# Steps from the 189th on in another order, with three masks more on VectorE and three fewer on GpSimd

## The chip, the cores and the metric

The kernel runs on one core of one Trainium2 chip. The metric is the device time of one execution in microseconds. The core has five engines with a queue of instructions each, in the order in which the program recorded them: TensorE (PE; its weight loads, PEld, are shown apart), VectorE (DVE), ScalarE (ACT), GpSimd (POOL) and SyncE (SP, which issues DMAs). An instruction waits at the head of its queue until what it depends on is done, and everything behind it in that queue waits too.

## The reference

Sliding-window attention with four sink tokens, then a perceptron with a squared relu over the 4 x 768 tokens:

```python
# q, k, v: 4 batches x 8 heads x 768 x 64, n_sink 4, window 128
keep = (pos[None, :] < n_sink) | ((rel >= 0) & (rel < window))   # rel = pos[:, None] - pos[None, :]
scores = np.where(keep, np.matmul(q, k.transpose(0, 1, 3, 2)) / np.sqrt(64), -1000000000.0)
a = np.exp(scores - np.max(scores, axis=-1, keepdims=True))
a = a / (np.sum(a, axis=-1, keepdims=True) + 1e-09)
x = np.matmul(a, v).transpose(0, 2, 1, 3).reshape(3072, 512)
h = np.maximum(x @ w_in, 0.0)          # w_in: 512 x 2048
out = (h * h) @ w_out                  # w_out: 2048 x 512
```

## The kernel before

The program is a table of 992 steps (`P.ops`): each is a small function that issues a few instructions on one engine. A string, `ORDER`, lists the numbers of the steps in the order in which `Plan.run` records them; a letter behind a number names the engine (p, d, a, g for PE, DVE, ACT, POOL; without a letter it is the first that the step allows), and `+0` or `+1` chooses between two pools of PSUM banks (`den` and `att`, two slots each). Slots of SBUF pools are given out in the order of the string too: eight `expm` slots (exponentials and the copies `t`), three `r`, four `sg`, two `osb`. So the string fixes each engine's queue and which slot a step takes; waits follow from the data and from the slots.

Attention of a batch b goes in three blocks s of 256 queries, and a block in two halves of two head pairs. For each half there are four kinds of step. *Scores* (L592 to L613) multiply k by q into `ps` in PSUM. *Expo* (L630, ScalarE) writes exp to `expm` as bf16. *Domask* (L635) zeroes what lies outside the window: in block 0 a product with `mask0` on VectorE (L639); in the others either a product with `tri` on VectorE (L642, one instruction of 1024 columns) or two selects on GpSimd (L218, 512 columns each). *Values* (L678) multiply by v and the sinks into `po`; *norm* (L694, L695, VectorE) divides into `xn_sb`. The choice of L635 to L643 is

```python
elif e == "dve":
    y = x.rearrange("p h (i c) -> p (h i) c", i=2)
    nc.vector.tensor_mul(y, y, tri.rearrange("p (o a) c -> p o (a c)", o=1).to_broadcast(
        [128, 4, 256]))
else:
    y = x.rearrange("p h (i g c) -> p g (h i) c", i=2, g=2)
    for i in range(2):
        triangles(y[:, i], i, 4)
```

The result is transposed to `xT` by TensorE and copies (b = 0, part of 1) or by DMA (`turn_x`); *spread* (L833) copies it into `xd`.

The first layer is done plainly for batch 0 (`layer1`, products L762, squares L785 and L787). From batch 1 on it is done with seven products in place of eight (Strassen's scheme in Winograd's form): sums `xs` of the input (L854) and `wi` of the weights, then `quad` (L867), seven products L892 into two PSUM banks `pm` (each four or eight loads of weights). Out of a quad come copies `t` of a product (*kept*, L192 on ScalarE or L194 on VectorE), *bounded* forms `r` = max(pm + t, 0) (L942, always VectorE), one relu (L967 ScalarE or L969 VectorE), and two *squares* into `gT_sb` (L915 ScalarE or L917 VectorE). A product that overwrites a bank waits for the copy or bounded form that reads it.

The second layer is plain for one block of batch 0 and otherwise again seven products: `layer2_chain` (L1194), products L1239 into `py`; ahead of them four sums of blocks of `gT_sb` on VectorE (L1213: s1 to `sg`, s3 in place in `gT_sb`, s2 and s4 to `sg`), behind them the quarters of the result to `osb`, as copies (L192 or L194) or additions (L1253), and one store. The third quarter's copy frees the region of `py` that the next product writes. The last block of batch 3 runs `layer2_fast` (L1035: sums L1058, products L1100 and others), interleaved with the chain of the block before.

Of the kernel before, what the change touches and what calls it, by code (L numbers as in the profile page):

```python
# [18 lines left out]


ORDER = """
990 1 0 2 7 8 9 10 11 12 13 14 15 16 17 18 56d 60a 55d 991+0 3 19 57+0 61d 20 5 6 4 62+1 65 59a 67+0 58a 21 64d 89d
63a 68+0 75+1 88d 69 70 76+1 22 71+0 77 23 72 73 78 24 94a 79+1 90+0 93d 92a 95+1 80 91d 81 96a 74 100+0 82 101+0 25
26 102 83+1 97d 66 84d 27 104 85 110+1 111+0 103g 86d 152+1 112 28 113d 105d 98+0 99 153 106+0 108 114 115d 154a 116+1
118 29 160+1 109 161 162a 107 30 119 117 120+0 31 155d 163a 122 121d 123d 32 168+0 156+1 331 33 172+0 157 169 164+1
170a 165 34 35 158d 173 166a 124+1 125a 127+0 36 159d 176+1 129a 177 126d 174a 140+1 133+1 37 128d 171d 142 136 180+1
181 282+0 38 178d 167d 137d 132+0 141+1 182a 130+0 39 283 40 144 143d 41 134 42 43 332 284 285 131 145d 146+0 175a 147
135g 278 179a 286 138+1 139 287 288 148+0 150 334 151d 44 149a 279 183d 289 184+1 290 185 193+0 280 281 200+0 201 291
194 45 204+1 196+0 202 46 203 205 198a 186 197 207a 293 206 187+0 199a 216+0+0 47 48 195a 217 49 188d 234+1+0 50 235
190+0 219 208+0 87 292 237 209 295 191 218 297+0 189 220 51 336 52 212 53 210a 294 211 255+0 252+1 254 299 298 256 54  # L30
253a 257 444 223+0+1 333 238d 445 192a 226 304 213 224 221+0 312 222 300 241+1+0 301 214+0 296 244 215 302 225 446
303d 242 306 260+0+0 236 462 263 307 314 337 316+0 245d 243d 315 227 308 313 447 318 319 464 246+0 261 247 239+0 448
240 320 321 228+0 475 322d 317 229 258+0 335 259 325 449 450 310 326 230+0 451 231 452 232 248+0 233 249a 327 250 251a
323 309 305 343+1 359+1 339 338 344 467 340 345 341 360 463 329 311 453 324 328 346 465 347 361 362 363 267+1+1 348
349 350 364 268 342 365d 270 351d 366 367 375+0 352 376 377 354 368 454 355 468 356d 370 369a 357 455 391+0 456 379
264 457 262 466 458 265+0 271 393 353 459 378 269 371 392 395 358a 266 372 272+0 373 381 380 382 474 374a 397 394 273
274+0 383d 276 277 396 275a 384 469 407 386 485+0+0 388d 718 472 387 470 460 486 398 410 461 408 389 412+1 488 471
478+1+0 409 399 473 385 479 400 487 330 413 688 402 414 428+0 404 401 403 405 430 416 429 418 432 406a 489 530+0 481
415 390 417 431 419 532 689 526 411 490+0 434 420 433 435 528 421 423 491 436 437 707 482 527 422a 533 424 480 534 690
708 476+0 477 425 439 440 441 691 535 442 531 483+1 426 529 484 443a 536 494+0+0 537 438a 497 692 427 495 568+0 545  # L40
539 540 570 564 566 492 693 694 695 542 498d 501+0+0 502 565 696 541 493 571 504 697 706 538 572 698 543 569 709
517+0+1 518 546 699 573 544 547 520 700 575 503d 510+0+0 701 574 549+0 496d 583 711 576 567 577 584 578 521d 513 505
579 585 551 581 506+0 552 580 507 514 511 586 512d 553 519 713 588+0 499+0 710 500 554 702 703 555d 515+0 516 522+0
589 719 550 590 712 523 591 745+0+0 748 592 558 556 548 560 746 738+0+0 741 594d 557 593 587 595 559 562 739 561
722+0+0 747 596d 714 604+0 749d 725 597 606 599 605 600 726 601 608 607 715 508 509 723 602 524 716 525 717 656+1 657
598 720+0 658 609 620 721 659 610 622 640+0 750+0 724 611 642 612 621 641 751 613 742 603a 660 662 740 615 644 623 646
614 727+0 616 704 661 617 663 563 643 645 618 647 619 672+0 664 667 665 648 651 649 728 582 674 668 673 669 650 676
670 743+0 652 666a 675 744 653 624+1 678 671a 677 654 626 679 625 729+1+0 680 730 628 770 681 655 630 683 774+0 771
732 684 627 775 685 686 629 772 776 754+0+1 682a 755 731 631 777 687 733 773 632 734+0 735 778 635 779 757 705 761+1+0
633 637 636 781 752 758 780d 634 762 638 756 639a 736 793+0 783 789 764 790 784 759+0 737 791 785 795 760 763 782 765  # L50
794 827 828 800 832+1 766+0 786 787 767 848+0 788 850d 829 833 808 796 834 835 830 849 797 768 836 838d 810 851 753
798 837 852 812+1 792 839 853 799 854 855 856 769 801 802 804 840d 859 803 841 857 831 814 843 815 858 842a 866 844
861 805d 816 845 811 809 806 860 817 868+0 813 862 864 846 819 865 818 863 869 870 884+1 867 871 821 872 885 874 823
886d 873 875 822 847 876 916+0 824 887 888 917 889 932 825 877 878 879 890 934 820 918 880 919 920 900+1 807 902 881d
882 933 891 921 883a 901 892 904 936+0 922d 938 906 903 923 905 893 924d 895 896 907 925 894a 897 939 935 908d 927 898
928 926a 940 929 937 826 911 909 899a 913 910 930 941 931 912 942 914 943 946 915 970 955+1 944 945 957 951 974+0 948
953 971 947 952 958 975 949 959d 956 972 960 950 961 973 977+0 962 976 978 964 954 966 979d 965 963 980 968 981 982
985 967d 969 983 984 989 986 988 987
"""
DUMMIES = {  # L60
    57: 9, 62: 14, 95: 7, 83: 3, 991: 29,
# [1348 lines left out]
```

## Time and profile before

| | |
|---|---|
| time, median of 3 runs | 209.87 us (209.62 to 209.92) |
| the profiled execution's own time | 209.26 us |
| its span | 207.6 us |
| mean granted TensorE clock | 1.00 |
| masks in blocks s > 0 and the first | 27 on VectorE (15 at L642, 12 at L639), 17 on GpSimd (34 selects) |

The profile names an instruction by line, engine, operation, tile written and tiles read. A row of the timeline has the start in us from the span's start, the time in us, then the instruction, how many follow one another (x), and in brackets the idle time of the engine ahead of it with what ended it; "issue" is time for which the profile shows no releaser. The row of a group of instructions has the shortest, median and longest duration in ns and the first and last start.

### The profile page before, as it was taken

The numbers are of one execution on the slowest core, as the hardware profiler recorded it, in microseconds if no ns is written. First come the engines' busy times: TensorE is split into PE (matmuls) and PEld (weight loads), VectorE is DVE, ScalarE is ACT, GpSimd is POOL, SyncE is SP. The second block draws the span as 40 slices with busy tenths as digits, with TensorE's granted clock in tenths as the row PEclk, the third lists the DMA queues.
The fourth block names the chain that finished last, engine by engine and source line by source line (L and its number), as shares of the span: only waits on it lengthen the run. The fifth ranks groups of instructions, "written<-read, shape, count | busy, mean of one in ns | idle before, by whom it ended". The sixth has DMA issues, their size and how long they took to land.

```text
span 207.6 us, 6021 instructions
## 1 busy us (share of the span) xinstructions
PE 199.6 (96%) x2500; PEld 176.2 (85%) x2502; DVE 174.7 (84%) x342; ACT 133.9 (64%) x208; POOL 96.2 (46%) x137
## 2 busy tenths in 40 slices
PE   7969999999899999999999999999999999999993
PEld 7458997579878899889878988998889999999893
DVE  4387657498899998999998778999989998998853
ACT  2769458729998168898888458989871452584010
POOL 7799275699499927999333529000280000000000
PEclk9999999999999999999999999999999999999999
DMA  5999999999999999999999996901023220200205
GB/s 157 220 218 200 186 185 212 180 156 175 159 75 126 147 129 225 117 182 155 123 142 235 103 135 194 115 3 25 12 42 129 53 94 10 104 0 0 104 0 202
DMA packets 96042, 26.10 MB, mean 126 GB/s; under 512 B 86800, under 2 KB 93456, under 8 KB 96016
## 3 DMA queue, kind: packets, MB, share of 16 engines
q0 software_dynamic: 69248, 12.59, 86.5%
q1 hardware_dynamic: 25568, 12.49, 27.2%
q10 hardware_dynamic: 1200, 0.66, 1.1%
q8 instruction: 19, 0.31, 0.6%
q14 instruction: 7, 0.06, 0.1%
HBM read 27.30 MB, written 6.29 MB: 162 GB/s over the span
## 4 chain that ended last, share of the span: by engine, by line
PE 80%; DVE 6%; ACT 6%; DMA 4%; issue 2%; POOL 0%; ACTq 0%; POOLq 0%; DVEq 0%
PE py L1239 28%; PE pm L892 25%; PE pm L762 9%; PE po L678 6%; PE ps L609 4%; DMA v<-in_v_dram 4%; PE py L990 3%; ACT expm L630 2%; PE py L1100 2%; PE pt L503 1%; DVE r L942 1%; ACT gT_sb L915 1%; PE px L727 1%; DVE xn_sb L695 1%; ACT qkT L192 1%
## 5 line engine op out<-in xcount | busy, mean ns | idle before, releaser
L630 ACT ACTIVATE expm<-ps 128x1024 bf16<-128x1024 f32 (+1 forms) x48 | 43.8, 951 | 9.6 <-PE ps L609 7.6
L218 POOL TENSOR_SCALAR_AFFINE_SELECT expm<-expm 128x512 bf16<-128x512 bf16 x34 | 24.0, 740 | 42.2 <-DVE xn_sb L695 19.5
L942 DVE CUSTOM_DVE_ANT_0 r<-pm,t 128x512 bf16<-128x512 f32 x54 | 36.0, 684 | 1.6 <-PE pm L892 1.2
L1239 PEld LDWEIGHTS <-gT_sb 128*128 128x128 bf16 x320 | 30.4, 98 | 4.4 <-issue 0.6
L892 PEld LDWEIGHTS <-w_in_sb 128*128 128x128 bf16 x384 | 32.4, 114 | 1.7 <-issue 1.5
L192 ACT ACTIVATE t<-pm 128x512 f32<-128x512 f32 x42 | 24.7, 600 | 13.4 <-PE pm L892 12.7
L892 PEld LDWEIGHTS <-wi 128*128 128x128 bf16 x288 | 24.7, 114 | 0.8 <-issue 0.7
L1239 PEld LDWEIGHTS <-sg 128*128 128x128 bf16 x240 | 22.5, 98 | 3.1 <-DVE sg L1213 0.3
L192 ACT ACTIVATE osb<-py 128x256 f32<-128x256 f32 (+1 forms) x36 | 14.1, 397 | 15.7 <-PE py L1239 15.0
L762 PE MATMUL pm<-xT,w_in_sb 128*128 128x256 bf16 x192 | 22.5, 273 | 0.1
L892 PE MATMUL pm<-xs,wi 128*128 128x256 bf16 (+1 forms) x192 | 21.6, 246 | 0.0
L892 PE MATMUL pm<-xs,w_in_sb 128*128 128x256 bf16 (+1 forms) x192 | 21.5, 246 | 0.0
L762 PEld LDWEIGHTS <-w_in_sb 128*128 128x128 bf16 x192 | 20.5, 114 | 0.8 <-issue 0.5
L1239 PE MATMUL py<-wt,gT_sb 128*128 128x256 bf16 x160 | 20.7, 273 | 0.2
L1239 PE MATMUL py<-wt,sg 128*128 128x256 bf16 x160 | 20.8, 273 | 0.0
L1239 PE MATMUL py<-w_out_sb,gT_sb 128*128 128x256 bf16 x160 | 20.4, 273 | 0.0
L915 ACT ACTIVATE gT_sb<-r 128x1024 bf16<-128x1024 bf16 x17 | 18.0, 1056 | 1.8 <-DVE r L942 1.6
L678 PE MATMUL po<-v,expm 128*128 128x65 bf16 x352 | 17.9, 193 | 1.1 <-DMA v<-in_v_dram 1.1
L678 PEld LDWEIGHTS <-expm 128*128 128x128 bf16 x352 | 16.8, 97 | 2.3 <-issue 1.3
L695 DVE TENSOR_TENSOR xn_sb<-po,rc 128x512 bf16<-128x512 f32 (+1 forms) x28 | 17.2, 615 | 1.0
L1253 DVE TENSOR_TENSOR osb<-py,osb 128x256 f32<-128x256 f32 x30 | 12.1, 416 | 4.7 <-PE py L1239 4.6
L609 PE MATMUL ps<-qkT 64*128 64x128 bf16 (+1 forms) x256 | 14.5, 238 | 1.1 <-ACT expm L630 0.6
(107 smaller groups left out, 377.8 us busy)
## 6 DMA issues: line engine op xcount, KB each, us to landing
out_dram<-osb SPq DMA_DIRECT2D x11, 512.0 KB, 3.0
v<-in_v_dram POOLq DMA_DIRECT2D x24, 128.0 KB, 7.0
qn<-in_k_dram POOLq DMA_DIRECT2D x20, 128.0 KB, 6.6
qn<-in_q_dram POOLq DMA_DIRECT2D x20, 128.0 KB, 6.3
w_in_sb<-in_moe_w_in_dram POOLq DMA_DIRECT2D x4, 512.0 KB, 9.2
w_out_sb<-in_moe_w_out_dram POOLq DMA_DIRECT2D x4, 512.0 KB, 10.5
qr<-in_k_dram SPq DMA_DIRECT2D x4, 256.0 KB, 6.9
qr<-in_q_dram ACTq DMA_DIRECT2D x2, 256.0 KB, 4.2
```

The lines of the kernel that those rows point to most:

```text
L192: return nc.scalar.activation(out=dst, in_=src, func=AF.Copy)
L218: nc.gpsimd.affine_select(out=e_tile, in_=e_tile, compare_op=ALU.is_ge, fill=fill, base=i - 1, pattern=[[0, n], [1 if i else -1, 128]], ch ...
L609: nc.tensor.matmul(ps[:, h2, o:o + w], lhsT=qkT_sb[r, m, 1, c, :], rhs=qkT_sb[r, m, 0, qb:qb + w // 128, :], start=(i == 0 and not biased) ...
L630: nc.scalar.activation(out=x[:, :, o:512], in_=bank_t["s", b, s, m][:, :, o:512], func=AF.Exp, scale=scale)
L678: touch(("po", b, s, m0), e, nc.tensor.matmul(pv[:, i, h2, :], lhsT=lhsT, rhs=rhs, start=(n_ == 0), stop=(n_ == len(mms) - 1)), j)
L695: touch(("po", b, s, m0), e, nc.vector.tensor_tensor(out=xn_sb[:, 2 * s:2 * s + 2, 128 * (m0 + j0):128 * (m0 + j0 + nj)].rearrange("p i (j ...
L762: nc.tensor.matmul(pm[:, i, :], lhsT=w_in_sb[:, fb // 4, kb, fb % 4:512:4], rhs=xT[:, c0 // 256:(c0 + cw) // 256, kb, :], start=(kb == 0), ...
L892: touch(tag, e, nc.tensor.matmul(y[:, bk, i, :], lhsT=weights(name, f0 + i, a), rhs=rhs[:, a, :], start=fresh and i == 0 and a == 0, stop= ...
L915: nc.scalar.activation(out=d, in_=x, func=AF.Square)
L942: touch(tag, e, nc.vector._custom_dve(TENSOR_ADD_SAT, out=d.rearrange("p n c -> p (n c)"), in0=T["y"][:, 1].rearrange("p n c -> p (n c)"), ...
L1239: touch((b, u), e, nc.tensor.matmul(region(name), lhsT=x[:, i, :], rhs=w_[:, i, :], start=first and i == 0, stop=i == HB - 1, skip_group_c ...
L1253: ins = nc.vector.tensor_tensor(out=d, in0=region(of), in1=d, op=ALU.add)
```

## The change

Only the string `ORDER` differs; it is four lines longer, so that a line of the kernel before has a number larger by 4 in the one after (L1213 becomes L1217). Most words of the new string carry a letter that the step would have had anyway. The first place at which the orders differ is the 189th of 992 steps, about 43.5 us into the span, and the last seven steps stand as before. `DUMMIES` and all functions are the same.

```diff
 ORDER = """
...
-928 926a 940 929 937 826 911 909 899a 913 910 930 941 931 912 942 914 943 946 915 970 955+1 944 945 957 951 974+0 948
...
+909d 938a 913a 939 910d 912 898d 929a 937 899a 914d 940a 915a 955+1 930d 931d 941 957a 943 942a 970d 951d 945d 971d
...
```

This is a line of each string from the last token blocks; all others from the 189th step on differ in the same manner.

Sixty steps change their engine. Nine of them are masks: six go from GpSimd to VectorE and three from VectorE to GpSimd, so that VectorE has 30 of 44 and GpSimd 14 (28 selects). The others, in the program's counts: copies `t` are 42 on ScalarE and 12 on VectorE before, 50 and 4 after; squares of L915 and L917 17 and 19 before, 23 and 13 after; relus of quads 15 and 3 before, 13 and 5 after; result copies 34 and 7 before, 32 and 9 after. TensorE has the same 2502 loads and products in another order.

The first place is about 149 to 156 us, where the sums for the second block of batch 2 are made while the last masks of batch 3 run. VectorE's queue of before, from the last bounded form ahead of the squares (`r`) through the sums (`sg`, `gT_sb` from `gT_sb`) to the norm (`rc`, `xn_sb`):

```order
L942 ISA r<-pm,t 128x512
L194 COPY osb<-py 128x256
L917 TENSOR_TENSOR gT_sb<-r 128x2x2x256
L942 ISA r<-pm,t 128x512
L1253 TENSOR_TENSOR osb<-py,osb 128x256
L1213 TENSOR_TENSOR sg<-gT_sb 128x1024
L1213 TENSOR_TENSOR gT_sb<-gT_sb 128x8x128
L1213 TENSOR_TENSOR sg<-sg,gT_sb 128x1024
L694 RECIPROCAL rc<-po 128x8
L695 TENSOR_TENSOR xn_sb<-po,rc 128x2x2x128
```

And the same stretch of VectorE's queue in the change, from the addition behind that bounded form to the mask of the last half block:

```order
L1257 TENSOR_TENSOR osb<-py,osb 128x256
L921 TENSOR_TENSOR gT_sb<-r 128x2x2x256
L1217 TENSOR_TENSOR sg<-gT_sb 128x1024
L1217 TENSOR_TENSOR gT_sb<-gT_sb 128x8x128
L1257 TENSOR_TENSOR osb<-py,osb 128x256
L1217 TENSOR_TENSOR sg<-gT_sb 128x1024
L198 COPY osb<-py 128x256
L858 TENSOR_TENSOR xs<-xd 128x256
L858 TENSOR_TENSOR xs<-xd,xs 128x256
L858 TENSOR_TENSOR xs<-xd 128x256
L1217 TENSOR_TENSOR sg<-sg,gT_sb 128x1024
L646 TENSOR_TENSOR expm<-expm,tri 128x1024
```

The last square ahead of the sums now stands on VectorE (before, it was on ScalarE); the sum s1 of the next block is moved up among them, the third sum is later, and a mask that GpSimd made stands behind the sums.

The second place is the tail, 184 to 194 us, on two engines. ScalarE's queue of before, from the last copies `t` of the last quads to the five result copies at the end:

```order
L192 ACTIVATE t<-pm 128x512
L915 ACTIVATE gT_sb<-r 128x2x2x256
L967 ACTIVATE r<-pm 128x512
L915 ACTIVATE gT_sb<-r 128x2x2x256
L192 ACTIVATE osb<-py 128x256
L967 ACTIVATE r<-pm 128x512
L915 ACTIVATE gT_sb<-r 128x2x2x256
L967 ACTIVATE r<-pm 128x512
L192 ACTIVATE osb<-py 128x256 x5
```

The same stretch of ScalarE's queue in the change:

```order
L196 ACTIVATE t<-pm 128x512
L919 ACTIVATE gT_sb<-r 128x2x2x256
L971 ACTIVATE r<-pm 128x512
L196 ACTIVATE t<-pm 128x512
L196 ACTIVATE osb<-py 128x256
L971 ACTIVATE r<-pm 128x512 x2
L919 ACTIVATE gT_sb<-r 128x2x2x256
L196 ACTIVATE osb<-py 128x256
L919 ACTIVATE gT_sb<-r 128x2x2x256
L196 ACTIVATE osb<-py 128x256 x5
```

A square now stands between the first result copy and the other five, where a relu stood. VectorE's queue at this place, before, with the last squares and bounded forms and the sums of the last two blocks (L1213 of the chain, L1058 of the last block):

```order
L942 ISA r<-pm,t 128x512
L917 TENSOR_TENSOR gT_sb<-r 128x2x2x256
L1058 TENSOR_TENSOR sg<-gT_sb 128x1024
L1253 TENSOR_TENSOR osb<-py,osb 128x256 x2
L1213 TENSOR_TENSOR sg<-gT_sb 128x1024
L1213 TENSOR_TENSOR sg<-sg,gT_sb 128x1024
L1058 TENSOR_TENSOR gT_sb<-gT_sb 128x8x128
L1213 TENSOR_TENSOR gT_sb<-gT_sb 128x8x128
```

And in the change:

```order
L946 ISA r<-pm,t 128x512 x3
L921 TENSOR_TENSOR gT_sb<-r 128x2x2x256
L1062 TENSOR_TENSOR sg<-gT_sb 128x1024
L1217 TENSOR_TENSOR sg<-gT_sb 128x1024
L1257 TENSOR_TENSOR osb<-py,osb 128x256
L1062 TENSOR_TENSOR gT_sb<-gT_sb 128x8x128
L1217 TENSOR_TENSOR gT_sb<-gT_sb 128x8x128
L1217 TENSOR_TENSOR sg<-sg,gT_sb 128x1024
L1062 TENSOR_TENSOR sg<-sg,gT_sb 128x1024
```

The chain's first sum is one addition earlier, its sum s2 (`sg` from `sg`) is behind both in-place sums, and one addition is later.

More of the change, by code (lines that the diff above doesn't have):

```diff
@@ L27 @@
[L27 to L46, printed above, removed]
@@ new lines @@
+153 106+0 108 114a 115d 154a 116+1 118 29g 160+1 109d 161 162a 107d 30g 119d 117d 120+0 31g 155d 163a 122 121d 123d
+32g 168+0 156+1 331d 33g 172+0 157 169 164+1 170a 165 34g 35g 158d 173 166a 124+1 125a 127+0 36g 159d 176+1 129a 177
+126d 174a 140+1 133+1 37g 128d 171d 142a 136a 180+1 181 282+0 38g 178d 167d 137d 132+0 141+1 182a 130+0 39g 283 40g
+144a 143d 41g 134a 42g 43g 332d 284 285 131a 145d 146+0 175a 147d 135g 278d 179a 286 138+1 139d 287 288 148+0 150 334d
+151d 44g 149a 279d 183d 289 290a 280d 184+1 291a 196+1 200+1 201 45g 197 185a 46g 47g 202a 204+0 293d 199a 205 48g
@@ new lines @@
+294d 295d 198a 49g 206d 193+1 50g 203d 281d 187+0 194a 51g 188d 186d 216+0+1 207a 217a 234+0+0 52g 296d 219a 190+0
+237a 208+0 209 87g 297+0 235a 218d 238d 220d 211d 212g 191a 210d 221+0 53g 222d 255+1 189a 252+0 299a 192d 298 256a
+253d 257d 254a 195d 54g 213a 300 223+0+1 292 312d 214+0 301a 314d 226a 302 236g 444g 313d 215a 303d 315d 445g 224a
+241+1+0 227d 336d 304 244a 307 225d 446g 447g 448g 242a 260+0+0 261a 316+0 317 228+0 309a 263a 245d 464 306d 318a 305d
+449g 308 243d 229d 239+0 246+0 462 310d 230+1 240d 465 232 247d 319 233d 248+0 250 450g 251d 320a 323 249d 321 231a
@@ new lines @@
+322a 339d 337d 341d 466 451g 343+1 359+1 452g 344 325d 345a 262d 468 258+1 453g 327 333d 340d 326 360 361a 324d 329d
+346d 259a 475a 328a 338d 454g 362d 342d 469 347 455g 363 267+1+1 335d 349a 348 365a 270a 474g 264d 350 364 375+0 351a
+268a 352d 354 366 356a 355 391+0 467 456g 376 463 367a 457g 370 377a 458g 353d 459g 357d 269g 392 271g 393a 368d 371
+379 265+0 372d 358a 373d 378d 266d 272+0 369a 381a 330 395 374a 397a 380 382 383a 274+0 273d 276 394d 275d 396 277a
+384d 470 407a 386 385d 485+0+0 387 486a 388d 488a 398 412+1 399a 389d 478+1+0 414a 413 471 402 408d 460g 410d 409d 416
@@ new lines @@
+400d 479a 428+0 403 472 404a 401d 461g 418a 429 415d 405d 430a 417 487d 489d 419 390a 406a 431d 481a 718g 420a 432
+530+0 526d 528d 411d 434a 532a 433 490+0 688g 473 423 421d 491d 689g 690g 435 533 425a 691g 436a 424 534a 437d 527d
+422a 311 480d 439 426d 441a 438a 692g 476+0 535 482d 440 536a 477a 531 706 537 483+0 442d 427a 529d 538d 494+1+0 693g
+443a 539d 540 484d 564d 541 495a 565d 707 694g 492 542a 543d 568+0 497a 566d 567d 501+0+1 695g 502a 570a 496d 569 504a
+517+0+0 503d 571 711 498d 572a 544 549+0 696g 573 545d 518a 505d 697g 575 698g 520a 546d 493 519d 574a 510+0+0 511a
@@ new lines @@
+577d 578 576d 709 699g 579 547d 700g 713 548d 701g 551d 513a 712 506+0 552 507d 702g 521g 553d 583a 514g 499+0 512g
+716 710 719a 554 500d 555d 522+0 580a 515+0 581d 588+0 708 589 584d 585d 550 523d 590a 559 516d 745+0+0 703g 746a 591d
+586d 508 558d 587d 592 594d 748a 593 560 595 715 562d 509 738+0+0 556 596a 597d 557d 599 600 741a 524 747g 525 561a
+601d 739a 604+0 714 722+0+0 602d 717 606a 725a 723a 605 598d 608 607d 656+1 620d 657 658a 726d 720+0 749g 721a 609
+659d 640+0 750+0 621d 740d 610a 622d 742g 603a 611 641 751d 612a 660 615 642a 644 617a 613d 616 724d 661 614d 662a
```

31 lines of the change are left out of this document (15 added, 16 removed).

## The prediction

> **What bounds the kernel now.** I read the page first: busy time, the slices, the chain of work that ended last.
>
> ```profile
> span 207.6 us, 6021 instructions
> PE 199.6 (96%) x2500; PEld 176.2 (85%) x2502; DVE 174.7 (84%) x342; ACT 133.9 (64%) x208; POOL 96.2 (46%) x137
> PE   7969999999899999999999999999999999999993
> PEclk9999999999999999999999999999999999999999
> PE 80%; DVE 6%; ACT 6%; DMA 4%; issue 2%; POOL 0%; ACTq 0%; POOLq 0%; DVEq 0%
> ```
>
> TensorE is busy for 96% of the span at the full granted clock, and four fifths of the chain are its own. GpSimd (POOL) has no share of the chain. VectorE at 84% is the next engine. So a new order can only win or lose what TensorE waits. The windows, cut by stage, show how little that is where the order differs, from about 44 us on (columns: window, its length, then busy time of PE, weight loads, DVE, ACT, POOL, clock, DMA share, GB/s):
>
> ```profile
> 44.40:66.00 21.60, 21.02 (x250) 18.40 (x249) 20.09 (x34) 18.31 (x28) 18.32 (x26) 1.00 1.95 139
> 66.00:90.00 24.00, 23.82 (x323) 21.52 (x322) 23.03 (x48) 16.46 (x28) 18.31 (x28) 1.00 1.96 160
> 90.00:128.00 38.00, 38.00 (x563) 33.44 (x562) 34.24 (x67) 29.29 (x47) 21.60 (x28) 1.00 1.72 142
> 128.00:156.00 28.00, 27.87 (x357) 25.18 (x356) 26.46 (x49) 23.98 (x37) 7.31 (x10) 1.00 0.32 61
> 156.00:180.00 24.00, 24.00 (x293) 22.96 (x292) 22.75 (x47) 8.91 (x18) 0.00 (x0) 1.00 0.22 69
> ```
>
> Idle TensorE in these five windows is 0.58 + 0.18 + 0 + 0.13 + 0 = 0.89 us by matmuls, whose ends are modelled. The queue of weight loads shows more, as it marks the starts; I take the waits from there:
>
> ```profile
> PEld L609 <- issue: 6.0, 23, 0.7
> PEld L1239 <- DVE gT_sb L1213: 0.4, 1, 0.4
> PEld L1239 <- DVE sg L1213: 0.3, 1, 0.3
> PEld L678 <- DVE expm L642: 0.2, 1, 0.2
> ```
>
> The first row is 23 stretches of scores at about 0.2 each, a cost of entering such a stretch: 26 stretches stand in the old order and 26 in the new, so this cost stays. Two larger waits also stay:
>
> ```profile
> 51.31 0.61 PEld L609 LDWEIGHTS <-qkT 64*128 64x128 bf16 x15 [0.20 <-issue]
> 52.62 0.17 PEld L609 LDWEIGHTS <-qkT 64*128 64x128 bf16 x5 [0.70 <-issue]
> 87.19 1.06 ACT L192 ACTIVATE xd<-xT 128x1024 bf16<-128x1024 bf16 x1 [0.40 <-DVE xT L194]
> 88.16 1.49 ACT L630 ACTIVATE expm<-ps 128x768 bf16<-128x768 f32 x2
> 89.00 0.45 PEld L892 LDWEIGHTS <-w_in_sb 128*128 128x128 bf16 x7 [0.31 <-issue]
> ```
>
> At 52.62 (0.70) the second score step of a stretch waits for a bank that an exponential must free. At 89.00 (0.31) a product waits for a bank held by an exponential that began late behind the `xd` copy. Both have the same neighbours in the new order. Removable, then, are three: 0.41 and 0.31 in rows below, and 0.07 at a product at 173.50:
>
> ```profile
> 173.50 0.93 PEld L1239 LDWEIGHTS <-gT_sb 128*128 128x128 bf16 x8
> ```
>
> Its eight loads take 0.93 against the 0.86 of such a row elsewhere. With scraps of 0.03 to 0.14 elsewhere that makes about 1.0 us: the ceiling of any gain.
>
> **The change part by part.** TensorE's instructions are the same 2502, in another order: 0. The loads of the others move: VectorE gets six masks and gives three back; eight copies `t` of a product net (12 to 4) and six squares of L915/L917 net (19 to 13) leave it for ScalarE.
>
> ```profile
> L642 DVE TENSOR_TENSOR expm<-expm,tri x15: 678/684/1112, 18.3 to 125.2; 128x1024 bf16<-128x1024 bf16 x15
> L218 POOL TENSOR_SCALAR_AFFINE_SELECT expm<-expm x34: 624/634/1137, 16.0 to 154.2; 128x512 bf16<-128x512 bf16 x34
> L917 DVE TENSOR_TENSOR gT_sb<-r x19: 680/683/986, 81.8 to 190.1; 128x1024 bf16<-128x1024 bf16 x19
> L915 ACT ACTIVATE gT_sb<-r 128x1024 bf16<-128x1024 bf16 x17 | 18.0, 1056 | 1.8 <-DVE r L942 1.6
> L192 ACT ACTIVATE t<-pm x42: 579/597/653, 74.7 to 182.9; 128x512 f32<-128x512 f32 x42
> ```
>
> Successors on VectorE start about 0.08 before the row's end, on ScalarE 0.10. So, from the order's counts, VectorE gets 3 x 0.60 = 1.8 us for masks and loses 8 x 0.60 + 6 x 0.60 = 8.4 (a `t` copy on it lasts like the 0.68 of a product's bounded form); two relus, two result copies and a square more of the first layer return some 2. That is -4.6 us. ScalarE gains 8 x 0.50 + 6 x 0.96 = 9.8, less some 2 for what it gives: +8. GpSimd loses six selects, 3.8 us. None of these sums is the time, since TensorE is the bound; they say that VectorE gets slack and that ScalarE (64%) loses some. What counts is who is late at each joint.
>
> **Joint one, about 149 to 155 us.** Here the square, two sums and GpSimd's masks meet:
>
> ```profile
> 149.10 4.01 POOL L218 TENSOR_SCALAR_AFFINE_SELECT expm<-expm 128x512 bf16<-128x512 bf16 x6 [19.47 <-DVE xn_sb L695]
> 150.78 0.68 DVE L942 CUSTOM_DVE_ANT_0 r<-pm,t 128x512 bf16<-128x512 f32 x1
> 151.55 1.06 ACT L915 ACTIVATE gT_sb<-r 128x1024 bf16<-128x1024 bf16 x1 [0.79 <-DVE r L942]
> 152.64 1.01 DVE L1213 TENSOR_TENSOR sg<-gT_sb 128x1024 bf16<-128x1024 bf16 x1 [0.83 <-ACT gT_sb L915]
> 153.69 1.07 DVE L1213 TENSOR_TENSOR gT_sb<-gT_sb 128x1024 bf16<-128x1024 bf16 x1
> 154.82 1.64 PEld L1239 LDWEIGHTS <-gT_sb 128*128 128x128 bf16 x16 [0.41 <-DVE gT_sb L1213]
> ```
>
> The square takes 1.06 on ScalarE, the first sum starts behind it and takes 1.01, the second 1.07, both stretched from 0.68 because a select runs beside them; then the product starts, 0.41 late. The new order puts this square on VectorE directly behind the bounded form `r` and one small add; the chain becomes 0.68 to 0.99 (the longest L917 row) in place of a handover of 0.09 and 1.06, so it ends 0.1 to 0.4 sooner, and one of the two masks that were beside the sums (`expm` of the next tile) goes to VectorE, behind both sums. If the sums run unstretched, another 0.33 + 0.39 is gained. The gain is capped by the wait: 0.41. I take 0.34, as other selects may still fall beside one sum.
>
> [...]
>
> **Joint two, the last sums, 186 to 194 us.**
>
> ```profile
> 186.65 1.05 ACT L915 ACTIVATE gT_sb<-r 128x1024 bf16<-128x1024 bf16 x1
> 188.72 0.38 ACT L192 ACTIVATE osb<-py 128x256 f32<-128x256 f32 x1 [0.22 <-PE py L1239]
> 190.06 0.69 DVE L917 TENSOR_TENSOR gT_sb<-r 128x1024 bf16<-128x1024 bf16 x1
> 190.59 0.86 PEld L1239 LDWEIGHTS <-gT_sb 128*128 128x128 bf16 x8
> 191.53 0.81 PEld L1100 LDWEIGHTS <-sg 128*128 128x128 bf16 x8
> 191.39 0.75 DVE L1253 TENSOR_TENSOR osb<-py,osb 128x256 f32<-128x256 f32 x2
> 191.78 0.66 ACT L192 ACTIVATE osb<-py 128x256 f32<-128x256 f32 x2 [2.67 <-PE py L1239]
> 192.77 0.69 DVE L1213 TENSOR_TENSOR sg<-sg,gT_sb 128x1024 bf16<-128x1024 bf16 x1
> 193.51 0.77 PEld L1239 LDWEIGHTS <-sg 128*128 128x128 bf16 x8 [0.31 <-DVE sg L1213]
> ```
>
> VectorE makes the last square at 190.06 and then five of the sums while ScalarE idles 2.67; the product at 193.51 waits 0.31 for the sum of 192.77, and the one at 191.53 starts 0.07 behind the end of the loads before it. The new order gives the last square but one to ScalarE and two earlier ones to VectorE, and more products stand ahead of the first reader of these sums. With products at 0.87 (eight loads) and 0.44 (four), operations of VectorE at 0.60, quarter additions at 0.33 (the 0.75 of two, less one of 0.42), ScalarE's square at 0.96 and copies at 0.28, and 0.3 from the last load of a product to the operation that reads it (the 0.28 of handover here), I placed the chain by hand: the sum ends just as its product is due, and no wait over 0.07 is left. Gain 0.38 - 0.07 = 0.31, between 0.38 and a loss that is priced below. The 0.07 near 173.5 goes as well.
>
> **What the new order may add.** It moves some 800 steps, and each place where an exponential, mask or square changes its neighbours can make a new wait; the trace of before cannot show these. Bounds: six masks on VectorE ahead of their value products, 0 to 0.2 each by the L678 row, so 0 to 1.2; six squares on ScalarE, 0 to the 0.41 of the row at 154.82 each, if each stood as that one does, 0 to 2.5; eight `t` copies with one more handover of 0.09 (from the `r` that ends at 151.46 to the square at 151.55), 0 to 0.7. Below nothing too, by the 0.2 to 0.3 of scraps that may go. I lean to the low end because 1.0 us in 160 is what all such joints cost now, and take 0.45: 0.15 from 44 to 66 us, where value products of one tile are moved forward to just behind their mask, 0.05 to 90, 0.1 to 128, and 0.15 to 155. No DMA changes its number; one load of q moves ahead of six selects on POOL's queue, so it is issued sooner by their 3.8 us, many steps before its transpose: 0.
>
> **Sum:** -0.34 - 0.31 - 0.07 + 0.45 = -0.27 us. From the profiled execution's 209.26 (207.6 and 1.66 around it) this gives 208.99. That execution lies 0.61 under the median of 209.87, so beside the median the forecast is 209.6.
>
> **The rivals.**
> *Fast:* the same removals, and nothing new. All removable waits go: 209.87 - 1.0 = 208.9. For it: VectorE's 4.6 us of slack, which sits where it was 90 to 96% busy in the five windows. Against: the 800 moved steps.
> *Slow:* ScalarE becomes late in the tail. In the new order two squares (1.05 each), relus and three result copies stand in its queue between two products of the last token blocks, and the copy that frees a quarter for the third product stands behind them all. If these follow without the 0.10 of overlap, or start 0.3 later, that product waits 0.8, the next 0.2, and the one that needs the last sum 0.3: 1.3 against the 0.38 saved, so 209.87 + 0.9 = 210.8. It decides from the moment at which that copy ends after the product ahead has issued its loads; by my placing it ends 0.2 sooner. For it: that margin is small. Against: the 2.67 of idle ScalarE there now.
> *Not what it says:* the masks move, but the sums meet other selects, as GpSimd keeps 28, so that joint one stays at 0.41; with the new waits paid by the tail it is 209.9.
>
> **How the numbers follow.** Forecast 0.47, fast 0.27, slow 0.16, not what it says 0.10. About 0.2%, 0.4 us, is what a measurement of this kernel can tell from no change. The forecast's own spread is -0.7 to +0.2, so 0.14 of its 0.47 is a visible gain and 0.03 a loss. Faster: 0.14 + 0.26 = 0.40. Slower: 0.03 + 0.15 = 0.18. Same: the remaining 0.42. The range runs from 208.7, a little past the fast case, to 210.6, which leaves out the worst of the slow case and the long ends of the unknown waits.
>
> **What would show it.** Right: the product that reads the second sum near 154 us with under 0.15 of wait, a square L917 ahead of the two sums; no wait over 0.1 at the products of the last 20 us; the 0.70 and 0.31 still there near 52 and 89; POOL with 28 selects. Wrong: a wait of the products on a copy or square of ScalarE between 184 and 190 us; new rows of value products waiting for L646 (the mask on VectorE) over 0.2; or sums at over 1.0 us beside selects again.

## The result, and the profile after

The change is slower: 212.70 us in the median of 4 runs (211.30 to 213.78) against 209.88 (209.62 to 209.92) of the kernel before, a ratio of 1.0131 (95% interval 1.0095 to 1.0166). On another occasion 12 runs of the same kernel gave 210.87 in the median (209.28 to 213.08) against 209.78, and a ratio of 1.0022 (0.9990 to 1.0054). Ratios leave out runs that lie over 1.5% above the fastest of their kernel; as the two profiles taken at such a time (213.78 here, 215.75 in e16 below) show waits of the kernel's own, I give medians and extremes beside the ratios. The spread is itself part of the result: before stays within 209.1 to 211.4 in all its runs, the change goes from 209.3 to 213.8.

The page of the change, the profiled execution being the run of 213.78 (rows as before: span, busy time, TensorE by slices, its clock, the chain by engine):

```profile
span 212.1 us, 6010 instructions
PE 202.4 (95%) x2500; PEld 179.2 (84%) x2502; DVE 170.0 (80%) x336; ACT 140.5 (66%) x217; POOL 91.0 (43%) x131
PE   7889999999999999999999995999999999999993
PEclk9999999999999999999999999699999999999999
PE 87%; DMA 4%; DVE 4%; ACT 2%; SPq 1%; issue 1%; DVEq 0%; ACTq 0%
```

VectorE lost 4.7 us of work and ScalarE gained 6.6, much as the counts said. But one slice of TensorE shows 5 and the next a clock of 6. The windows about it (columns as in the prediction):

```profile
128.00:129.80 1.80, 1.80 (x26) 1.68 (x24) 1.69 (x5) 1.80 (x4) 1.40 (x2) 1.00 0.46 65
129.80:132.60 2.80, 0.25 (x3) 0.00 (x0) 2.36 (x5) 0.45 (x1) 0.00 (x0) 1.00 1.73 211
132.60:136.10 3.50, 3.46 (x39) 2.84 (x40) 0.00 (x0) 2.15 (x3) 0.00 (x0) 0.52 0.83 245
136.10:140.00 3.90, 3.90 (x60) 3.86 (x58) 3.40 (x7) 2.71 (x6) 0.00 (x0) 0.99 0.00 0
```

TensorE's queue starts nothing for 2.8 us while DMAs are busy (0.25 of it is the end of earlier products), and then its granted clock is 0.52 for 3.5 us, which costs 3.5 x 0.48 = 1.7 us more. In shorter windows the clock is 0.50 throughout from 132.80 to 136.10, and 1.00 from 136.20 on. The rows show that the fall came behind the wait, not what made it.

What it waited for, in the waits of the change (engine, line, what for: total, times, longest):

```profile
PE pk L572 <- DMA qkT<-qn: 2.6, 1, 2.6
PEld L572 <- issue: 3.5, 5, 2.8
PEld L682 <- DVE expm L646: 0.2, 1, 0.2
```

L572 (L568 before) multiplies the sink keys of batch 3 by q, and needs every DMA transpose of k and q of that batch (`qkT` from `qn`, issued by SyncE). No value product waits over 0.2 for a mask on VectorE. SyncE's queue of before, and then of the change, shows the transposes of k and q among those of `xn_sb` to `xT`:

```profile
117.95 4.53 SPq L709 DMA_TRANSPOSE xT<-xn_sb  x3
122.57 1.22 SPq L460 DMA_TRANSPOSE qkT<-qn  x1
123.85 1.26 SPq L709 DMA_TRANSPOSE xT<-xn_sb  x1
125.22 1.20 SPq L460 DMA_TRANSPOSE qkT<-qn  x1
```

```profile
122.59 3.88 SPq L713 DMA_TRANSPOSE xT<-xn_sb  x3
126.56 2.53 SPq L464 DMA_TRANSPOSE qkT<-qn  x2
129.21 1.03 SPq L1286 DMA_DIRECT2D out_dram<-osb  x2
127.63 1.77 POOL L418 DMA_DIRECT2D v<-in_v_dram  x2
132.61 0.13 PEld L572 LDWEIGHTS <-kblk 128*32 128x32 bf16 x4 [2.82 <-issue]
```

Before, the last such transpose has been issued by 126.42. In the change it is the second of a pair issued until 129.09, and GpSimd has begun two loads of v at 127.63; the product starts at 132.61, 3.5 us after the pair was issued, though its turn had come at 129.79.

The two joints of the prediction went much as said. At the sums (VectorE, then TensorE's queue of weight loads):

```profile
156.94 0.68 DVE L921 TENSOR_TENSOR gT_sb<-r 128x1024 bf16<-128x1024 bf16 x1
157.72 0.69 DVE L1217 TENSOR_TENSOR sg<-gT_sb 128x1024 bf16<-128x1024 bf16 x1
158.45 0.69 DVE L1217 TENSOR_TENSOR gT_sb<-gT_sb 128x1024 bf16<-128x1024 bf16 x1
157.83 3.40 PEld L1243 LDWEIGHTS <-gT_sb 128*128 128x128 bf16 x32
```

The square is on VectorE, both sums are unstretched, and four products follow without a gap; the 0.41 is gone. In the tail the products stand one behind the other:

```profile
197.04 0.86 PEld L1104 LDWEIGHTS <-sg 128*128 128x128 bf16 x8
198.03 0.77 PEld L1243 LDWEIGHTS <-sg 128*128 128x128 bf16 x8
198.81 0.86 PEld L1243 LDWEIGHTS <-gT_sb 128*128 128x128 bf16 x8
```

The product that waited 0.31 starts 0.13 behind the loads before it. A further 0.9 us comes at the start: the scores that begin at 35.91 before begin at 36.80 here, in steps that both kernels have alike. These parts add up to more than the 4.5 us between the two spans, since the change also gains, as shown further below.

### The profile page after: what moved, and what is told of

Same layout as the page of the kernel before. It is cut to its first block, busy times and chain, and to the rows that moved or that the text cites. A ratio compares the mean times of both kernels' runs of the same rounds, so it can differ in the third digit from the quotient of the medians.

```text
span 212.1 us, 6010 instructions
## 1 busy us (share of the span) xinstructions
PE 202.4 (95%) x2500; PEld 179.2 (84%) x2502; DVE 170.0 (80%) x336; ACT 140.5 (66%) x217; POOL 91.0 (43%) x131
## 4 chain that ended last, share of the span: by engine, by line
PE 87%; DMA 4%; DVE 4%; ACT 2%; SPq 1%; issue 1%; DVEq 0%; ACTq 0%
PE py L1243 29%; PE pm L896 25%; PE pm L766 9%; PE po L682 7%; PE ps L613 5%; PE py L994 3%; PE pt L507 3%; DMA qkT<-qn 2%; DMA qr<-in_q_dram 2%; PE py L1104 2%; ACT expm L634 1%; PE px L731 1%; DVE qs L198 1%; PE ps L606 1%; SPq L713 1%
## 5 line engine op out<-in xcount | busy, mean ns | idle before, releaser
L222 POOL TENSOR_SCALAR_AFFINE_SELECT expm<-expm 128x512 bf16<-128x512 bf16 x28 | 18.5, 688 | 52.8 <-ACT expm L634 42.6
L196 ACT ACTIVATE t<-pm 128x512 f32<-128x512 f32 x50 | 28.3, 604 | 13.3 <-PE pm L896 12.1
L896 PEld LDWEIGHTS <-w_in_sb 128*128 128x128 bf16 x384 | 33.1, 115 | 1.7 <-issue 1.2
L919 ACT ACTIVATE gT_sb<-r 128x1024 bf16<-128x1024 bf16 x23 | 24.0, 1062 | 2.0 <-DVE r L946 1.9
L196 ACT ACTIVATE osb<-py 128x256 f32<-128x256 f32 (+1 forms) x34 | 13.6, 401 | 16.4 <-PE py L1243 16.4
L766 PEld LDWEIGHTS <-w_in_sb 128*128 128x128 bf16 x192 | 20.5, 114 | 0.9 <-issue 0.5
L896 PE MATMUL pm<-xs,wi 128*128 128x256 bf16 (+1 forms) x192 | 21.1, 246 | 0.0
L682 PEld LDWEIGHTS <-expm 128*128 128x128 bf16 x352 | 17.3, 99 | 1.3 <-DVE expm L646 0.2
```

What stands on the lines that cost most here:

```text
L196: return nc.scalar.activation(out=dst, in_=src, func=AF.Copy)
L222: nc.gpsimd.affine_select(out=e_tile, in_=e_tile, compare_op=ALU.is_ge, fill=fill, base=i - 1, pattern=[[0, n], [1 if i else -1, 128]], ch ...
L682: touch(("po", b, s, m0), e, nc.tensor.matmul(pv[:, i, h2, :], lhsT=lhsT, rhs=rhs, start=(n_ == 0), stop=(n_ == len(mms) - 1)), j)
L766: nc.tensor.matmul(pm[:, i, :], lhsT=w_in_sb[:, fb // 4, kb, fb % 4:512:4], rhs=xT[:, c0 // 256:(c0 + cw) // 256, kb, :], start=(kb == 0), ...
L896: touch(tag, e, nc.tensor.matmul(y[:, bk, i, :], lhsT=weights(name, f0 + i, a), rhs=rhs[:, a, :], start=fresh and i == 0 and a == 0, stop= ...
L919: nc.scalar.activation(out=d, in_=x, func=AF.Square)
```

## The experiments

All edits move words of the string `ORDER` or change their engine letters; each diff shows a moved number with a neighbour, without its letter. The table has every run; "half" counts runs with a mean clock of 0.993 or less, about what one spell at half clock leaves: the run of 213.78, which lost 1.7 us to its spell, has 0.990. The runs counted have 0.977 to 0.992, all others in the table 0.997 or more; below, a run with a halved clock is one with such a mean, which does not show where the clock fell (two of the four runs of the first measurement, and two of all runs of before, have it).

| run | edit, on which order | median (lowest to highest), runs | before there | ratio (95%) | half |
|---|---|---|---|---|---|
| e1 | change, transposes early | 210.50 (209.44 to 212.81), 12 | 209.84 | 1.0021 (0.9998 to 1.0044) | 0 |
| e2 | before, transpose late | 209.65 (209.03 to 210.54), 10 | 209.84 | 0.9992 (0.9972 to 1.0012) | 0 |
| e3 | before, masks of the change | 211.58 (211.10 to 213.41), 7 | 209.84 | 1.0085 (1.0055 to 1.0115) | 0 |
| e4 | change, v early | 209.98 (209.52 to 213.48), 10 | 209.84 | 1.0000 (0.9980 to 1.0021) | 2 |
| e5 | e1, layer one ahead | 210.70 (209.68 to 218.82), 12 | 209.91 | 1.0041 (1.0017 to 1.0066) | 1 |
| e6 | change, layer one ahead | 211.10 (209.72 to 216.16), 10 | 209.91 | 1.0055 (1.0027 to 1.0084) | 1 |
| e7 | e5, masks of before | 220.02 (219.23 to 221.21), 4 | 209.91 | 1.0491 (1.0452 to 1.0530) | 4 |
| e8 | e2, v early | 211.02 (210.65 to 212.44), 10 | 209.91 | 1.0063 (1.0040 to 1.0087) | 1 |
| e9 | e1 and e4 | 210.71 (209.55 to 212.76), 12 | 209.62 | 1.0034 (1.0012 to 1.0057) | 0 |
| e10 | e9, a mask of batch 0 | 211.00 (209.76 to 211.98), 7 | 209.62 | 1.0067 (1.0033 to 1.0100) | 1 |
| e11 | e9, old start, store early | 209.47 (209.09 to 210.53), 12 | 209.78 | 0.9986 (0.9964 to 1.0008) | 0 |
| e12 | the change again | 210.87 (209.28 to 213.08), 12 | 209.78 | 1.0022 (0.9990 to 1.0054) | 2 |
| e13 | e9, store early | 210.07 (209.18 to 215.91), 12 | 209.78 | 1.0001 (0.9978 to 1.0023) | 2 |
| e14 | e11, a value product later | 209.93 (209.28 to 210.85), 12 | 209.71 | 1.0009 (0.9989 to 1.0029) | 0 |
| e15 | e14 without moves on DMA queues | 211.64 (209.47 to 216.49), 12 | 209.71 | 1.0047 (1.0019 to 1.0075) | 3 |
| e16 | old first 480, three moves | 215.43 (208.75 to 216.64), 6 | 209.62 | too few left in | 4 |
| e17 | old first 414, three moves | 210.42 (209.58 to 210.77), 6 | 209.62 | 1.0020 (0.9991 to 1.0049) | 0 |

### Late transposes, and the loads beside them: e1, e2, e4, e8

e1 moves three transposes ahead of the first one of `xn_sb` in SyncE's queue. The expectation calls all three q's; 708 and 709 are, but 710 is one of k, and the last pair stays where it was:

```diff
+708 709 710
 492
...
-709
...
-710
...
-708
```

> The changed kernel with three transposes of q for batch 3 (two for the first block, one for the second) issued on SyncE ahead of the first xT transpose of batch 2, where that queue stood idle; nothing else. Theory Q (SyncE's queue: in the new order the last two transposes of k and q stand behind four xT transposes, so the sink scores of batch 3 wait 2.8 us and the clock is halved for 3.4 us after it): the wait at the sink scores falls under 0.3 us, the granted clock is 1.00 in all runs, and the time is about 209.0 (208.6 to 209.6), under the kernel before. Theory M (the masks and the other moved work of VectorE and ScalarE cost the time, the wait at the sink scores only takes up what would wait later): 211 or more, with the waits at products or values. Theory C (the transposes are late because the loads of v run beside them): the wait shrinks too, since they leave that stretch; this run does not tell Q from C.

Its profile has no such wait: 0.20 at the sink scores is the usual entry.

```profile
125.08 2.53 SPq L464 DMA_TRANSPOSE qkT<-qn  x2
129.85 0.10 PEld L572 LDWEIGHTS <-kblk 128*32 128x32 bf16 x4 [0.20 <-issue]
```

No run has the halved clock (the means are 0.998 or more), and the median is 2.2 us under the first measurement of the change, but only 0.4 under the second (e12). It does not fall under the kernel before, as theory Q had it: something else is left.

e4 leaves SyncE as in the change and issues the loads of v 10 us sooner:

```diff
 703
+704 705
...
-704
...
-705
```

> The changed kernel with the two last loads of v for batch 3 issued some 10 us earlier on GpSimd's queue, behind the last load of q, so that they do not run beside the last transposes. Theory Q: the wait at the sink scores stays at 2 us or more and the time at 211 to 214. Theory C: the wait falls under 1 us and the time under 210.5.

Eight of ten runs lie at 209.5 to 210.3, and the profile waits 0.27 at the sink scores with the transposes issued as late as in the change (until 129.28): they landed within 1.3 us, against 3.5. The two others, 213.21 and 213.48, have the clock at 0.99, as two of the twelve runs of the unaltered change in e12 have. One profile without the wait is no proof, as e12's has none at this place either; it fits theory C, that the loads beside the transposes make most of the wait, which Q alone denied.

e2 does the lateness alone, in the order of before:

```diff
-714
...
 525
+714
 717
```

> The kernel before with only two transposes of batch 3 (the last one but two of k and the last of q) moved on SyncE's queue behind the last xT transpose of batch 2, as they stand in the change. Theory Q: the sink scores wait 1 to 3 us and the time is 211 to 213.5, with or without a halved clock behind it. Theory M: no effect beyond 0.3 us, 209.9.

Only 714 moves, as 717 stands there in the order of before too. It costs nothing: the pair was issued until 127.39, and the sink scores start on time at 129.39. e8 adds the early loads of v to it (704 and 705 behind 525). Its theory D, used from here on, is that the new order lets TensorE come to places where DMAs have not landed:

> The kernel before with the two transposes moved behind the last xT transpose (which alone cost nothing) and the two last loads of v issued some 4 us earlier on GpSimd, so that they run beside these transposes. Theory D: late and beside the loads together make the sink scores wait 1 us or more: 210.8 to 213.5. If position alone or loads alone decide it: 209.5 to 210.2.

```profile
124.33 1.77 POOL L414 DMA_DIRECT2D v<-in_v_dram  x2
125.36 2.50 SPq L460 DMA_TRANSPOSE qkT<-qn  x2
130.53 0.13 PEld L568 LDWEIGHTS <-kblk 128*32 128x32 bf16 x4 [1.20 <-issue]
```

The wait is there, 1.2 us where 0.2 is usual, and the kernel before becomes 1.1 us slower: all ten runs lie at 210.65 or above, those of e2 at 210.54 or below. So lateness alone is harmless (e2), and with the loads it is not (e8); the early loads alone, in the order of before, were not run. Theory Q falls as stated.

What differs in the profiles is which is issued first. The time from issue to landing (us, last column) of the last transpose of batch 3, in the first profile of the change and then in the second (e12), and the loads of v in the second:

```profile
qkT<-qn SPq DMA_TRANSPOSE x1, 4.6
qkT<-qn SPq DMA_TRANSPOSE x1, 2.4
128.54 1.77 POOL L418 DMA_DIRECT2D v<-in_v_dram  x2
```

In the first profile the loads of v start at 127.63, 0.2 us ahead of that transpose; in the second 0.9 behind it, and the sink scores do not wait. Where these loads start ahead of it or within 0.2 us behind, it takes 3.5 to 4.8 us (the change, e3, e7, e8); where they start 0.7 or more behind it, or have landed, it takes 2.4 to 2.5 in all profiles but one. That one is e16, with 4.0 and no such load beside it, so the loads of v are not the only cause of a late landing.

### The masks: e3 and e7

e3 gives the order of before the nine masks' engines of the change, and e7 gives a mended order of the change those of before:

```diff
-264 262 505 519 740 763
-521d 512d 749d
+264d 262d 505d 519d 740d 763d
+521g 512g 749g
```

> The kernel before, in its own order, with the nine masks on the engines of the change (six from GpSimd to VectorE, three back). Theory Q: within 0.4 us of 209.87, since no transpose moves. Theory M: slower by 1 us or more, with VectorE late at value products or sums.

Slower by 1.7 us. The profile of e3, first TensorE and then VectorE:

```profile
83.48 0.11 PEld L678 LDWEIGHTS <-expm 128*128 128x128 bf16 x2 [1.54 <-DVE expm L642]
81.11 0.68 DVE L942 CUSTOM_DVE_ANT_0 r<-pm,t 128x512 bf16<-128x512 f32 x1
81.70 1.72 DVE L642 TENSOR_TENSOR expm<-expm,tri 128x1024 bf16<-128x1024 bf16 x2
```

Two masks stand behind VectorE's other work in the old order, and the value product waits 1.54 for them. The same profile waits 0.79 at the sink scores, where the last transpose is issued 2.6 us later than before (127.81 against 125.22) and the loads of v at 127.96 come beside it. In the change the wait of 1.54 is not there; so the masks need the new order, and neither half of the change can be judged by itself.

> The kernel with both moves, in the order of the change, with all nine masks on the engines of before (six back to GpSimd, three back to VectorE). If the masks carry the gain of the new order (VectorE's sums unstretched): slower than the run with both moves by 0.3 to 1.0 us, with sums at 1.0 us beside selects again. If the squares and copies given to ScalarE carry it: the same within 0.3 us.

Both expectations of e7 were far off: 220.02. Its profile:

```profile
109.48 2.21 POOL L222 TENSOR_SCALAR_AFFINE_SELECT expm<-expm 128x512 bf16<-128x512 bf16 x2 [9.92 <-issue]
116.26 1.77 POOL L406 DMA_DIRECT2D qn<-in_k_dram  x2
138.56 0.11 PEld L572 LDWEIGHTS <-kblk 128*32 128x32 bf16 x4 [7.24 <-DMA qkT<-qn]
```

A mask that goes back to GpSimd stands there ahead of loads of k and q. Its queue waits for the mask's exponential, the loads of k start at 116.26 in place of 99.42 in the change, and the sink scores wait 7.2 us. So in this order the masks on VectorE also keep GpSimd's queue of loads free, which no count of busy time shows.

### What was left of the loss: e5, e6, e9, e10 and the second profile

> The changed kernel with two moves: the three early transposes of q on SyncE as in the first run, and on TensorE the layer-one step of four feature blocks that the change put behind the transposes of batch 1 put back ahead of the second of them (the one that waited 0.6 and 1.5 us for a load of q in two runs). Theory D (the change lets TensorE and SyncE come to two places where DMAs have not landed; all else of the change is a small gain): no wait over 0.3 us at these two places, the clock 1.00 in every run, and 209.0 to 209.5, about 0.5 under the kernel before, with a spread no wider than that of before. Rival N (the new order is no gain anywhere; what it wins at the sums it loses in small waits): 209.8 to 210.2.

> The changed kernel with the TensorE move of the run before alone; SyncE as in the change. Theory D: the sink scores of batch 3 still wait, 1 to 3 us, 211 to 213.5, in part of the runs with the clock at 0.99. If the transposes of batch 1 were the whole of it: 209.0 to 209.8.

Both move one layer-one step (193) from behind the transposes of batch 1 to between the first two:

```diff
 200
+193
 201
...
-193
```

The wait for q is gone, but the move makes one of its own: the layer-one step behind it waits 0.83 in both profiles. So e5 says nothing of the order's worth; one of its runs, 218.82, has a halved clock (0.984) though the three transposes are early. And e6, whose profile did not wait at the sink scores, is inconclusive but for its run of 216.16.

> The changed kernel with the three early transposes on SyncE and the two last loads of v issued early on GpSimd, both at once. Theory D: neither lateness nor the loads of v are left at the sink scores, so no run has the halved clock or lies above 212; what is left of the loss is the wait of 0 to 1.5 us for a load of q at the transposes of batch 1: 209.3 to 210.4. If the sink scores were not the cause of the runs at 213: some of the runs still lie there.

No run of e9 has the halved clock (0.997 or more), as theory D says, and one (212.76) lies above 212 all the same. The profile has two waits on DMAs:

```profile
PEld L507 <- DMA qn<-in_q_dram: 0.8, 1, 0.8
115.79 0.42 DVE L198 COPY osb<-py 128x256 f32<-128x256 f32 x1 [1.56 <-DMA out_dram<-osb]
116.27 0.75 PEld L1243 LDWEIGHTS <-sg 128*128 128x128 bf16 x7 [1.26 <-issue]
```

The first is the load of q for batch 1. The second is new: a result copy needs a slot of `osb` that the first store of batch 1 still reads, and the product behind it waits 1.26. e10 gives the mask ahead of that load of q to VectorE (135d ahead of 147d):

> As the run before, and one mask of batch 0 given from GpSimd to VectorE (which stands idle there, ahead of a norm), so that the load of q behind it on GpSimd's queue starts about 1.6 us sooner. Theory D: the wait at the transposes of batch 1 goes as well, and the time falls under that of the kernel before: 209.0 to 209.5. Rival N: no gain over the run before, 209.8 or more.

The load did not start sooner, first in e9 and then in e10:

```profile
40.51 0.89 POOL L375 DMA_DIRECT2D qn<-in_q_dram  x1 [0.34 <-DMA w_out_sb<-in_moe_w_out_dram]
```

```profile
40.69 0.88 POOL L375 DMA_DIRECT2D qn<-in_q_dram  x1 [1.53 <-DMA w_out_sb<-in_moe_w_out_dram]
```

Without the mask GpSimd waits that much longer for an earlier load to finish. So the load of q is not hurried in that way. The profile did not wait at the transposes; its start was late (the scores of 35.91 begin at 37.05). One run, 211.98, has the halved clock (0.992).

> The changed kernel once more, unaltered, for the spread of its runs on the chip of the other runs and for a second profile. Theory D: runs in two groups, about 213.5 where the sink scores of batch 3 wait over 2 us and the clock is halved behind it, and 210.5 to 212 where the wait is shorter; in the second profile the waits stand at the transposes of batch 1, at the first store's slot or at the sink scores, in sizes of their own, while the waits between engines are those of the first. Rival N: one group about 212.7 and the same waits.

The runs spread as theory D said, with two at 213 and a halved clock (0.992 in both), and the waits of the second profile are others than those of the first:

```profile
47.58 0.73 PEld L507 LDWEIGHTS <-qn 128*128 128x128 bf16 x13 [0.65 <-DMA qn<-in_q_dram]
122.70 0.34 PEld L613 LDWEIGHTS <-qkT 64*128 64x128 bf16 x10 [1.17 <-DMA qkT<-qn]
```

Nothing at the sink scores this time, but 1.17 at scores of batch 3 for another of its transposes, and 0.65 for the load of q. The first profile, with its late start, does not have the latter.

### The order without these waits: e11, e13, e14, e15, e16, e17

e11 takes the first 226 steps from before, and for the rest the change with three moves: transposes (e1), loads of v (e4), and the store ahead of a transpose:

```diff
+544
 711
...
-544
```

> The first 226 steps in the order of before (so the transposes of batch 1 come as late as there), the rest in the order of the change, with three moves on the DMA queues: the three transposes of q early on SyncE, the two last loads of v early on GpSimd, and the first store of batch 1 ahead of a transpose of k on SyncE. Theory D: no wait on a DMA over 0.3 us is left behind 45 us, and the time is 0.3 to 0.8 under the kernel before: 208.9 to 209.5. Rival N: 209.6 or more without such a wait.

> The changed kernel with the three moves on the DMA queues and its own first 226 steps. Theory D: as the run with the old start, plus the wait for the load of q at the transposes of batch 1, 0.6 to 1.5 us when the loads at the start are not late: 209.5 to 210.4.

e11 has the lowest median of all kernels here, 0.3 under before, but its interval takes in 1. Its profile waits on no DMA behind 45 us; its one new wait is for a mask, at a value product where old and new order are joined:

```profile
57.23 0.24 PEld L682 LDWEIGHTS <-expm 128*128 128x128 bf16 x6 [0.81 <-DVE expm L643]
```

e13, with the start of the change, waits 0.9 for the load of q in its profile and lies 0.6 above e11 and 0.8 under e12, the change of the same series; but two of its runs have the halved clock, 210.24 (0.992) and 215.91 (0.990). e14 puts that value product (221, with its norm 222) behind two transposes (252), e15 is the same without the three moves:

> The run with the old start and three moves, and one value product of batch 1 moved behind two transposes of batch 1 on TensorE; it waited 0.7 us there for its mask, because old and new order were joined ahead of it. Theory D: no wait over 0.3 us is left behind 45 us but the 0.7 at the scores near 53, and the time is 0.5 to 1.0 under the kernel before: 208.8 to 209.3 where that is 209.8. Rival N: no different from before within 0.2.

> The same without the three moves on the DMA queues (transposes of q, loads of v, first store as in the change). Theory D: the waits of the change come back at the scores, the store's slot or the sink scores of batch 3, in different sizes from run to run: 0.7 to 2 us above the run with the moves, and single runs near 213 with a halved clock. If the start (the transposes of batch 1) was the whole loss: the same as the run with the moves.

e14 misses: the product still waits 0.5 and scores behind it 0.5. But e14 and e15 differ only in the moves on SyncE and GpSimd, and that is 209.3 to 210.9 against 209.5 to 216.5, medians 209.93 and 211.64: there the three moves are worth 1.7 us in the median, and without them the spread is back. With the start of the change they do not take it away wholly (e13). Over the runs that keep the change's order (e7, e16 and e17 left out), the halved clock is in 10 of 48 with the transposes late and in 4 of 79 with them early.

> The first 480 steps (to about 95 us) in the order of before, the rest in the order of the change, with the three moves on the DMA queues. It keeps the change's order at the sums near 155 us and in the tail, and leaves out its waits at the transposes and value products of batch 1. Theory D: no wait on a DMA behind 45 us, the waits of before at 72, 89 (0.3 each or less) and 53 (0.7) still there, the 0.4 at 155 and the 0.3 at 193 gone, 0.4 to 0.9 under the kernel before. Rival N: no different from before within 0.2.

> The same with the first 414 steps in the order of before (to about 87 us). Theory D: as the run before, 0.4 to 0.9 under the kernel before, if the join of the two orders adds no wait of its own. Rival N: no different from before within 0.2.

Neither beats the kernel before. e16 shows the matter at its sharpest: one run at 208.75, the fastest of all kernels here, and five at 214.8 to 216.6; its profile waits again at the sink scores for transposes, those of the last pair, which no move touches, with no load of v beside them:

```profile
134.57 0.10 PEld L572 LDWEIGHTS <-kblk 128*32 128x32 bf16 x4 [2.73 <-DMA qkT<-qn]
```

e17 is 0.8 above before in the median and its interval takes in 1. No kernel here is shown to beat the one before.

## Why the prediction was wrong

**The bound** held: TensorE is the bound, and only its waits count.

**The two joints** held: 0.41 is gone and 0.31 is down to 0.13, in the way given (sums of 0.69 in place of 1.01 and 1.07, a square next to them, the tail's chain just in time), and the 0.70 near 53 us stayed. A select beside a sum did not stretch it everywhere: the second sum of the change took 0.69 though selects ran from 158.65 on, and in the kernel before the sum at 107.19 took 0.68 with one beside it from 107.23, that select 1.08 to 1.14 in place of 0.63. The 0.31 near 89 us, which the prediction says stays, is the usual 0.20 in the change (at 89.52). The slow rival did not happen: ScalarE idles 2.25 us in one stretch of the tail and no product waits for it.

**What the new order may add between engines** was taken at 0.45 of 0 to some 4 us. In the first profile of the change, from 44 us on, no wait of the queue of weight loads is over 0.25 but the 0.70 and those at 132 to 134 us, so that term came to about nothing. A sum over profiles estimates the whole of the engines' part. Less its late start (0.9), the wait on the DMA (2.6 and 0.2 behind it) and the half clock (1.7), the span of 212.1 leaves 206.7. The same for the second profile of the change (208.8 less 0.65 and 1.17), for e4 (208.5 less 1.5 and 0.1) and for e9 (209.0 less 0.8 and 1.26) leaves 207.0, 206.9 and 206.9, against 207.6 of before. So the engines' part is a gain of about 0.6 to 0.9, where -0.27 was forecast: right in sign, short in size. The ceiling of 1.0 held. This is an estimate from single profiles; no kernel without these waits was measured as faster.

**The DMAs** are the step that failed. The prediction says: "No DMA changes its number; one load of q moves ahead of six selects on POOL's queue, so it is issued sooner by their 3.8 us, many steps before its transpose: 0." It asked only whether loads on GpSimd come sooner, and never looked at SyncE's queue, where one transpose (714) went from ahead of four others to behind them, beside the one that stood there already, and the last of the pair was issued until 129.09 in place of 126.42; nor at the two loads of v that then start just ahead of it, nor at what TensorE now reaches sooner: the transposes of batch 1 and the slot of a result. In the first profile that term is not 0 but 2.8 for the wait and 1.7 for the clock; in others 0.6 to 2.1. None of the rivals had a DMA in it, though the page of before has this row, the busy share of the DMA engines in 40 slices:

```profile
DMA  5999999999999999999999996901023220200205
```

They are busy for nine tenths and more up to 125 us, and the waits on DMAs came there or soon behind it (132.61 in the change, 138.56 in e7).

**That the change does what it says** held: GpSimd has 28 selects, and the product with the two sums starts on time.

What stays open: why runs of one kernel differ in which DMA is late, why e16's last transpose was late without a load of v, and what halves the clock in the runs that have the moves. The profiles show one run each; that late transposes and loads of v together cost time is shown by e2 and e8 for one place, that the DMA queues carry the loss by e14 and e15, and competition elsewhere is only inferred.

## What to carry to other kernels

When an order is changed, walk the DMA queues as closely as the engines: for each transfer on a queue, what stands ahead of it now, what it runs beside, and how long before its reader it lands. In this kernel, with TensorE busy for 96%, an order that looks better by the engines' durations spent the slack in the landing times of transfers; measure such a kernel in many runs, as the loss comes in some of them. Look also for a mask, or another step that waits, in the same queue as loads: in e7 GpSimd stood idle for 9.92 us ahead of two selects, and the loads of k behind them started 17 us later than in the change.

## What the runs showed of the hardware

- A wait of TensorE of 2.8 us was followed by 3.5 us at a clock of 0.52; after the 1.2 us in e8's profile the clock stayed at 1.00.
- The last of a pair of DMA transposes landed within 1.3 us of the end of its issue with two stores and no load beside it (e4), after 3.5 us with two loads of v issued ahead of and beside it (the change), and after 2.8 us in e16 without such loads.
- The start differs from run to run: in the profiles of the change, e10, e15 and e17 the same steps came later than in the other profiles: the scores that follow 35 us began at 36.80 to 37.05, against 35.85 to 36.30 in the others.
